# Moving one of the shifted copies of VectorE's softmax tiles to GpSimd in a planned attention + MLP kernel

## The chip, the cores and the metric

The kernel runs on one core of a Trainium2 chip. The metric is the device time of one execution in microseconds (us). The profiles show single executions; engines are called PE (TensorE matmul), PEld (TensorE weight load), DVE (VectorE), ACT (ScalarE), POOL (GpSimd) and SP (SyncE, which issues DMAs).

## What is computed

A transformer block with adaptive layer norm: 2048 rows, width 512, 32 heads of 16, an MLP of width 1376. Cut to what matters:

```
mod = silu(c) @ w_mod                        # sa, ca, ga, sb, cb, gb: six rows of 512
h = layernorm(x) * (1 + ca) + sa
q, k, v = split_heads(h @ wqkv)              # 32 heads of 16
p = softmax(q @ k.T * 16 ** -0.5)            # per head, 2048 x 2048
x = x + ga * (merge_heads(p @ v) @ wo)
h = layernorm(x) * (1 + cb) + sb
x = x + gb * (gelu(h @ w1 + b1) @ w2 + b2)   # the result
```

All inputs and the output are bf16.

## The kernel before, in words

**Runs, tiles, blocks.** The attention is cut into 32 runs, each with 512 queries x 4 heads (the last eight: 256 queries x 8 heads). A run walks over 16 key tiles of 128 keys; a key tile is four score blocks of 128 keys x 512 columns, one for each group of 32 rows of PE. Scores stand in PSUM with keys on the partitions, and after the exponential they are the moving operand of the value matmuls (`pv_op`, line 975), which add into one PSUM bank for the run (`od`). A column of ones beside V gives the softmax denominators.

**Two ways to the exponential.** ScalarE takes score blocks in groups of three and two (`qk_a`, line 837, then the Exp at line 886). VectorE takes whole key tiles (`qk_d`). For each of a tile's four blocks it makes one first pass (`ph`, line 927): it reads PSUM and writes int16 numbers whose bits, read as bf16, are a straight-line stand-in for the exponential. When the tile is whole, `shifts` (line 937 on) adds four shifted copies of it (`sh`, line 942), each one instruction over 2048 int16 columns, and the five versions go through the value matmuls with five scalings of V (the `VX` tiles, made on GpSimd at line 771), so that the errors of the five average out. A VectorE tile thus has five groups of value matmuls where a ScalarE tile has one.

**Who takes which tile.** `DKS = (2, 6, 10, 14)` are the tiles of a run that VectorE may take. ScalarE takes the twelve others and, when these are done, those of the four that VectorE has not reached (`next_tile`).

**What sets the order.** The kernel is emitted by a list scheduler that runs when the kernel is built (`Plan`). Each step is an `Op` with an engine, an assumed duration, dependencies, a priority and buffers (`Res`) to take and give back; the scheduler keeps one model clock per engine, picks at each step the op that can start first (among near ones by `dyn` and a pseudo-random term from `SEEDS`, one seed for each 25 us), and emits it. The order on each engine is fixed by that; at run time the engines wait for each other by semaphores. Where PE has nothing to do in the model, `heat` emits matmuls on zeros (lines 445, 461 and 966).

**GpSimd beside VectorE.** GpSimd work that is cut into pieces (the normalising at line 1027, the scaling of weights by their gates at line 1050) is of kind "beside": the scheduler starts a piece only when VectorE is at an op that is not marked `port` (the copies `sh` are marked, the first passes not) and that has at least 0.5 us left (`Plan.beside`). `after_dve` makes the piece wait for the VectorE instruction before the last one emitted.

**The other parts.** Layer norm, projections and MLP of the four row blocks are spread among the runs; `block_tail` does output projection, second layer norm and MLP of a row block, and `last_half` the last 256 rows after the last run. The gelu works in place on `g`; the last chunk of `g` (96 of 128 partitions are used) gets ones in its spare partitions (`ones`, line 1148), so that the last W2 matmul adds b2. `late_loads` fetches weights in the first run, among them `WoP`, two regroupings of the last rows of Wo that only `last_half` uses (line 1281).

Of the kernel before, what the change touches and what calls it, by code (L numbers as in the profile page):

```python
# [25 lines left out]
NPH = 5  # L26
# [34 lines left out]
AL = 0.055  # L61
FILL = 2.1
SPREAD = 0.15
SEEDS = (189, 218, 297, 155, 171, 163, 261, 540, 974, 172, 672, 279, 663, 728, 301, 465, 719, 329, 508, 485, 116, 24, 319, 395, 351, 431, 815, 192, 264, 111, 379, 921)
HEAT = 1.7


# [8 lines left out]
class Op:  # L76
    count = 0

    def __init__(self, eng, fn, us, deps=(), lat=0.14, prio=5.0, mode=None, kind="", acq=None,
                 rel=(), gate=None, port=False):  # L80
        self.port = port
        self.eng, self.fn, self.us, self.lat, self.prio = eng, fn, us, lat, prio
        self.mode, self.kind, self.acq, self.rel, self.gate = mode, kind, acq, rel, gate
        self.end = None
        self.ready = 0.0
        self.tile = None
        self.slot = None
        self.kb, self.due, self.extra = 0, 1e9, False
        self.uses, self.use = 0, 1.0
        self.rows, self.cont, self.run = None, False, None  # L90
        self.waiters = []
        self.todo = 0
        self.seq = Op.count
        Op.count += 1
        for d in deps:
            if d is None:
                continue
            if d.end is None:
                d.waiters.append(self)
                self.todo += 1  # L100
            else:
                self.ready = max(self.ready, d.end)
        for owner in rel:
            owner.uses += 1
# [165 lines left out]
def kernel(  # L270
# [28 lines left out]
    EPS = 1e-5  # L299
    QSC = 0.25 * 128.0 / math.log(2.0)  # L300
    ESC = math.log(2.0) / 128.0
    DKS = (2, 6, 10, 14)
    NPT = 4
    FEW = 1
    MM = 0.2155
    SPAN = (3, 2)
    POOL_US, POOL_MIN = 0.68, 0.5
    A_US = {1: 0.49, 2: 0.9165, 3: 1.3435}
    AHEAD = 3
    PSUM_F = 11  # L310
    FIRST_DKS, D_TIME = (14,), 8.0

    psum = bass.MemoryType.PSUM
# [8 lines left out]
    def res(name, n, shape, dt, pool=work):  # L322
        return Res(name, n, lambda i: pool.tile(shape, dt, name=f"{name}{i}"))
# [5 lines left out]
    r_ax = res("ax", 2, [P, QB], FP32, pp)  # L329
    r_pt = [res(f"pt{n}_", NPT, [P, n * QB], BF16) for n in SPAN]  # L330
    r_ph = res("ph", 4, [P, 4 * QB], I16)
    r_sh = res("sh", 4, [P, 4 * QB], I16)
    r_xb = res("xb", 2, [P, TPB, D], BF16)
    r_blk = res("blk", NQ, [P, NC, D], BF16)
    r_w = res("w", 3, [P, NC, D], BF16)
# [22 lines left out]
    urgent = set()  # L358
    aux_at = [0.0]

    def dyn(plan, o):
        if o.eng == "DVE" and o.run is not None and (
                o.run < a_run[0] or o.run == a_run[0] and not own[o.run]):
            return 0.05
        if o.eng != "PE":
            return o.prio
        same = (-0.5 if o.mode[0] == plan.mode else 0.0) - 0.2 * o.cont
        if o.kind == "qkA":
            back = n_a[0] - n_a[1]
# [106 lines left out]
    sc = const.tile([P, NC], BF16, name="sc")  # L476
    modA = const.tile([P, 2 * NC], FP32, name="modA")
    modB = const.tile([P, 2 * NC], FP32, name="modB")
    ga_bc = const.tile([P, D], FP32, name="ga_bc")
    gb_bc = const.tile([P, D], FP32, name="gb_bc")  # L480
    qmask = const.tile([P, 2], FP32, name="qmask")
    Wo = keep.tile([P, NC, D], BF16, name="Wo")
    WoP = keep.tile([P, 2, D], BF16, name="WoP")
# [415 lines left out]
    def qk_d():  # L899
# [24 lines left out]
        def ex(e):  # L924
            n_d[1] += 1
            units[0] += 1
            nc.vector.tensor_scalar(out=ph.tile[:, o.row * QB:(o.row + 1) * QB], in0=o.tile, scalar1=PH_B,  # L927
                                    scalar2=0.0, op0=ALU.add, op1=ALU.max)
        d_e.append(op("DVE", ex, 0.6, (o,), lat=DL, prio=0.5, rel=(o,)))
        d_e[-1].run = r  # L930
        if last:
            shifts(r, kt, ph, list(d_e))

# [3 lines left out]
    def shifts(r, kt, first, es):  # L937
        def parts(o):
            return lambda: [o.tile[:, h * QB:(h + 1) * QB].bitcast(BF16) for h in range(4)]
        pv_op(r, kt, 0, es, parts(first), (first,))  # L940
        for j in range(1, NPH):
            sh = op("DVE", lambda o, j=j: nc.vector.tensor_scalar(  # L942
                out=o.tile, in0=first.tile, scalar1=PH_SH[j], scalar2=None, op0=ALU.add),
                0.6, es, lat=DL, prio=2.0, acq=r_sh, rel=(first,), port=True)
            sh.run = r
            pv_op(r, kt, j, (sh,), parts(sh), (sh,))

    def pv_op(r, kt, ph, deps, srcs, owners):
        cc, par, hb = run_heads(r)
# [127 lines left out]
    def late_loads(after):  # L1077
# [10 lines left out]

        def wo(o):
            nc.sync.dma_start(out=Wo, in_=A_wo.rearrange("(c p) f -> p c f", p=P))  # L1090
            wo_src = A_wo[(NC - 1) * P:NC * P, :].rearrange("(r p d) f -> r p d f", r=4, p=2)
            for r in range(4):
                for p in range(2):
                    nc.sync.dma_start(out=WoP[32 * r:32 * r + 16, p, :], in_=wo_src[r, p])
        z1 = op("POOL", lambda o: nc.gpsimd.memset(WoP, 0.0), 0.9, d, prio=8.0)
        o_late["wo"] = dma(wo, (z1,), kb=640, n=9)
        z2 = op("POOL", lambda o: (nc.gpsimd.memset(W1[:, :, F:NF * P], 0.0),
                                   nc.gpsimd.memset(b1_bf, 0.0),
                                   nc.gpsimd.memset(W2c[:, 2, :], 0.0)), 1.5, d, prio=8.0)
# [14 lines left out]
                          (o_late["small"],), prio=3.0)  # L1114

    W2 = {}

    def gate_bc(dst, w, kind):
        def bc(o):
# [51 lines left out]
    def block_tail(b, nt=TPB):  # L1171
# [19 lines left out]
        if part:  # L1191
            g.uses += 1
            x2.uses += 1
            held["x"] = x2
            o_late["part"] = g
            one = ones(g, (g,))
        ev = []
        if part:
            open_banks()
# [11 lines left out]
        if part:  # L1211
            ge = [op("ACT", lambda o, lo=lo, hi=hi: nc.scalar.activation(  # L1212
                out=g.tile[:, lo:hi, 0:N], in_=g.tile[:, lo:hi, 0:N], func=ACT.Gelu_apprx_tanh),
                0.2 * (hi - lo) * nt / 2 + 0.1 + 1.3 * (lo == 0), ev[lo:hi], lat=0.15, prio=0.5,
                gate=finished) for lo, hi in ((0, 2), (2, PSUM_F))]
# [5 lines left out]
        if part:  # L1221
            due(1e9)
        prev = None
        for t in range(nt):
            mm = chain([(lambda ps, t=t, f=f: w2_mm(ps, g.tile, t * P, f, f + 1), MM)
                        for f in range(NF)], (prev, one, o_late["w2"]), "part" if part else kind, r_ax, (g,), 3,
                       lambda f: ge[0] if not part else ge[f >= 2] if f < PSUM_F else ev[f])
# [14 lines left out]
    def last_half():  # L1242
# [15 lines left out]
        for n, t in enumerate(tiles):  # L1258
# [19 lines left out]
            def wo2(o, t=t):  # L1278
                for p in range(2):
                    at = p * HB + (t % 2) * P  # L1280
                    nc.tensor.matmul(out=acc[t].tile, lhsT=OT.tile[:, at:at + P], rhs=WoP[:, p, :], start=False,
                                     stop=(p == 1))
            w = op("PE", wo2, 2 * MM, (ml, early[t]), lat=PEL, mode=full, kind="last", prio=0.2)
# [25 lines left out]
            for f in range(NF):  # L1309
                def w1(o, f=f, at=at):  # L1310
# [3 lines left out]
                mm = op("PE", w1, 4 * 0.064, hd, lat=PEL, mode=full, kind="last", acq=r_t, prio=0.3)  # L1314
                gd.append(op("ACT", lambda o, f=f, mm=mm, gs=gs: nc.scalar.activation(
                    out=g.tile[0:rows(f), f, gs], in_=mm.tile[0:rows(f), 0:P], func=ACT.Gelu_apprx_tanh,
                    bias=b1c[0:rows(f), f:f + 1], scale=1.0), 0.265, (mm,), prio=0.3, rel=(mm,)))
            first = prev = None
            for f in range(NF):
                def w2(o, f=f, gs=gs):  # L1320
                    w2_mm((first_of[id(o)] or o).tile, g.tile, gs.start, f, f + 1)
                o = op("PE", w2, MM, (gd[f], prev), lat=PEL if f == NF - 1 else 0.0, mode=full,
                       kind="last", acq=r_ax if f == 0 else None, prio=0.4)
                first_of[id(o)] = first
                first = first or o
# [40 lines left out]
    def want_q(g):  # L1366
        while q_made[0] < g and q_made[0] + 1 < NQ * NC:
# [4 lines left out]
            due(1e9)  # L1372
            if cc == NC - 1:
                o_h[b].uses -= 1

    state = {"late": 0}
    qk_a()
    want_q(1)
    while True:
# [7 lines left out]
        while ended:  # L1387
# [13 lines left out]
            if r == 0:  # L1401
                late_loads(o_last[0])
                o_late["ga"] = gate_bc(ga_bc, o_late[2], "gate")
                o_late["wo"] = scaled([lambda u=u: Wo[:, u, :] for u in range(NC)] +
                                      [lambda p=p: WoP[:, p, :] for p in range(2)], ga_bc,
                                      (o_late["wo"], o_late["ga"]))
                lt = {3: o_late[3], 4: o_late[4]}
                gt = o_late["g"]
# [15 lines left out]
            if r == 6:  # L1424
# [43 lines left out]
```

## Time and profile before

| | us |
|---|---|
| median of three runs | 783.03 (781.84 to 783.94) |
| the profiled execution | 783.1 |
| its span, first to last instruction | 781.3 |
| busy in it: PE, DVE, ACT, POOL | 746.6, 737.4, 755.3, 124.5 |
| key tiles done by VectorE | 476 first passes / 4 = 119 of 512 |

A row of the costliest groups has the line, engine, operation, tiles (out<-in), their shapes and the count, then busy us and the mean ns of one, then the engine's idle time ahead of them and what ended it. Busy time merges what overlaps, so it can be less than count times mean. In the timeline a row is a start, a length, an engine, and a count of merged neighbours. In the table by stage, each engine has its busy us in the stretch.

### The profile page before, as it was taken

Reading aid. Unit: us, or ns where it says so; the run is one execution under the profiler, and the core shown is the slowest. Engines: PE = TensorE matmul, PEld = TensorE weight load, DVE = VectorE, ACT = ScalarE, POOL = GpSimd, SP = SyncE. Lnnn points to the kernel's source line nnn. Section 1 sums busy time; section 2 is a strip of 40 time slices with the busy share of each in tenths; the row PEclk is TensorE's granted clock in tenths of the full one; section 3 lists DMA queues with packets and bytes.
Section 4 is the critical chain, followed back from the end, with each engine's and each line's share of the span. In section 5 each row is a group of like instructions: output and inputs, shape, how many; then the busy total and the mean of one; then the engine's idle time right before and its main releaser. Section 6 shows DMA issues by size and latency. Waiting matters only on the chain.

```text
span 781.3 us, 21165 instructions
## 1 busy us (share of the span) xinstructions
PE 746.6 (96%) x8617; PEld 273.2 (35%) x8617; DVE 737.4 (94%) x1288; ACT 755.3 (97%) x680; POOL 124.5 (16%) x279
## 2 busy tenths in 40 slices
PE   8999999999999999999999999999999999999997
PEld 3433333333333222223322233222233444434455
DVE  6889987999999999999999999999999999999994
ACT  4899999999999999999999999999999999999994
POOL 6611124021224300010000200000000100010100
PEclk9999999999999999999999999999999999999999
DMA  7143001100020101010100010000111101010100
GB/s 215 36 117 106 19 23 47 24 22 9 13 74 23 25 22 46 17 23 6 44 19 22 25 26 20 20 22 24 31 46 31 26 18 46 18 24 18 26 18 28
DMA packets 38547, 27.73 MB, mean 35 GB/s; under 512 B 17941, under 2 KB 33846, under 8 KB 38450
## 3 DMA queue, kind: packets, MB, share of 16 engines
q1 hardware_dynamic: 38442, 26.39, 12.5%
q8 instruction: 67, 1.10, 0.6%
q14 instruction: 30, 0.25, 0.1%
q10 hardware_dynamic: 8, 0.00, 0.0%
HBM read 20.77 MB, written 2.61 MB: 30 GB/s over the span
## 4 chain that ended last, share of the span: by engine, by line
PE 34%; DVE 28%; ACT 26%; issue 8%; DMA 2%; SPq 1%; POOL 1%; DVEq 0%; ACTq 0%
ACT pt L886 24%; DVE sh L942 11%; DVE ph L927 11%; PE od L975 11%; PE st L837 10%; PE ax L1141 3%; PE ax L837 3%; PE ax L716 2%; PE ax L1202 2%; PE od L461 1%; DVE OD L1000 1%; DVE ln_s L621 1%; PE ax L1135 1%; DMA xb<-in_A_x_dram 1%; PE ax L755 1%
## 5 line engine op out<-in xcount | busy, mean ns | idle before, releaser
L886 ACT ACTIVATE pt<-st 128x1536 bf16<-128x1536 f32 x629 | 714.2, 1308 | 2.2 <-PE st L837 1.0
L927 DVE TENSOR_SCALAR ph<-ax 128x512 int16<-128x512 f32 x476 | 310.4, 682 | 8.0 <-PE ax L837 6.8
L942 DVE TENSOR_SCALAR sh<-ph 128x2048 int16<-128x2048 int16 x476 | 312.6, 694 | 2.1 <-PE od L975 0.9
L837 PE MATMUL st<-qm,kT 32*128 32x512 bf16 x1572 | 246.4, 383 | 16.0 <-ACT pt L886 12.4
L975 PE MATMUL od<-sh,VX 128*32 128x512 bf16 (+1 forms) x2400 | 167.4, 340 | 3.6 <-DVE sh L942 2.8
L837 PE MATMUL ax<-qm,kT 32*128 32x512 bf16 x476 | 158.9, 379 | 3.3 <-DVE ph L927 1.6
L837 PEld LDWEIGHTS <-kT 32*128 32x128 bf16 x2048 | 77.2, 91 | 233.6 <-issue 224.3
L975 PE MATMUL od<-pt,VEB 128*32 128x512 bf16 (+1 forms) x1960 | 141.8, 340 | 0.1
L975 PEld LDWEIGHTS <-VX 128*32 128x32 bf16 x2400 | 60.0, 95 | 84.6 <-issue 72.9
L975 PEld LDWEIGHTS <-VEB 128*32 128x32 bf16 x2560 | 62.9, 96 | 75.5 <-issue 59.4
L1027 POOL TENSOR_TENSOR OT<-OD,RB 128x256 bf16<-128x256 f32 x38 | 27.4, 732 | 320.4 <-DVE sh L942 207.3
L975 PE MATMUL od<-ph,VEB 128*32 128x512 bf16 (+1 forms) x600 | 46.9, 338 | 1.0 <-DVE OD L1000 0.7
L1202 PE MATMUL ax<-blk,W 128*128 128x512 bf16 (+1 forms) x176 | 44.1, 355 | 0.7 <-DVE ph L927 0.4
L461 PE MATMUL od<-warm 128*32 128x512 bf16 x440 | 41.7, 381 | 0.0
L716 PE MATMUL ax<-blk,w 128*128 128x512 bf16 x124 | 36.7, 382 | 1.3 <-DVE blk L640 0.6
L771 POOL TENSOR_SCALAR VX<-VEB 128x128 bf16<-128x128 bf16 x64 | 23.6, 369 | 89.2 <-DVE VEB L647 85.5
L1027 POOL TENSOR_TENSOR OS<-OD,RB 128x256 bf16<-128x256 f32 x24 | 17.2, 729 | 127.0 <-DVE sh L942 111.7
L1141 PE MATMUL ax<-w,g 128*128 128x512 bf16 x128 | 34.6, 381 | 1.8 <-ACT g L1212 1.0
L1207 DVE TENSOR_SCALAR g<-ax,b1c 128x512 bf16<-128x512 f32 (+1 forms) x44 | 29.2, 675 | 0.3 <-PE ax L1202 0.2
L621 DVE BATCH_NORM_STATS2 ln_s<-xb 128x6 f32<-128x512 bf16 x32 | 21.7, 678 | 2.8 <-DMA xb<-in_A_x_dram 2.7
L1141 PEld LDWEIGHTS <-g 128*128 128x128 bf16 x176 | 13.9, 97 | 24.1 <-issue 12.2
L1000 DVE COPY OD<-od 128x512 f32<-128x512 f32 x31 | 21.1, 681 | 0.2 <-PE od L975 0.2
(106 smaller groups left out, 375.8 us busy)
## 6 DMA issues: line engine op xcount, KB each, us to landing
RB<-rn SPq DMA_DIRECT2D x124, 64.0 KB
xb<-in_A_x_dram SPq DMA_DIRECT2D x7, 512.0 KB
out_dram<-o SPq DMA_DIRECT2D x16, 128.0 KB
qm<-qs SPq DMA_DIRECT2D x120, 16.0 KB
W<-in_B_w_dram SPq DMA_DIRECT2D x1, 1376.0 KB
w<-in_A_wqkv_dram SPq DMA_DIRECT2D x3, 384.0 KB
blk<-in_w_mod_dram SPq DMA_DIRECT2D x2, 512.0 KB
g<-in_w_mod_dram SPq DMA_DIRECT2D x2, 512.0 KB
```

The source lines that it names most:

```text
L461: nc.tensor.matmul(out=o_od[r].tile[32 * i:32 * i + 32, :], lhsT=warm[:, 0:32], rhs=warm[:, 0:1].to_broadcast([P, QB]), start=False, stop= ...
L621: nc.vector.bn_stats(out=st6, in_=src)
L716: return chain([(lambda ps, j=j: nc.tensor.matmul(out=ps[:, 0:QB], lhsT=w.tile[:, j, cc * P:(cc + 1) * P], rhs=o_h[b].tile[:, j, :], start ...
L837: nc.tensor.matmul(out=o.tile[:, k * QB:(k + 1) * QB], lhsT=kT[cc][kb][rows, ko * P:(ko + 1) * P], rhs=qm.tile[rows, par, :] if hb is None ...
L886: nc.scalar.activation(out=e.tile[:, 0:len(got) * QB], in_=o.tile[:, 0:len(got) * QB], func=ACT.Exp, scale=ESC)
L927: nc.vector.tensor_scalar(out=ph.tile[:, o.row * QB:(o.row + 1) * QB], in0=o.tile, scalar1=PH_B, scalar2=0.0, op0=ALU.add, op1=ALU.max)
L942: sh = op("DVE", lambda o, j=j: nc.vector.tensor_scalar(out=o.tile, in0=first.tile, scalar1=PH_SH[j], scalar2=None, op0=ALU.add), 0.6, es, ...
L975: nc.tensor.matmul(out=o_od[r].tile[32 * i:32 * i + 32, n * HB:n * HB + w], lhsT=v_tile(kt, ph)[:, c0:c0 + 32], rhs=got[i][:, at:at + w], ...
L1027: two = beside(lambda c: nc.gpsimd.tensor_tensor(out=OT.tile[:, c], in0=OD.tile[:, c], in1=o5.tile[:, c], op=ALU.mult), (OT,), (OD, o5), f ...
L1141: nc.tensor.matmul(out=ps, lhsT=g[:, f, col:col + P], rhs=rhs, start=(f == 0), stop=(f == NF - 1))
L1202: mm = chain([(lambda ps, f=f, j=j, f0=f0: nc.tensor.matmul(out=ps[:, (f - f0) * N:(f - f0 + 1) * N], lhsT=W1[:, j, f * P:(f + 1) * P], rh ...
L1207: ev.append(op("DVE", lambda o, f=f, f0=f0, mm=mm: nc.vector.tensor_scalar(out=g.tile[:, f, 0:N], in0=mm.tile[:, (f - f0) * N:(f - f0 + 1) ...
```

## The change

- For a VectorE tile, the last of the four shifted copies is now made on GpSimd (`by_pool`): four pieces of 512 int16 columns, each after the first pass that it reads, of kind "beside", with 0.65 us in the model, into one buffer `sg`. This is done after 60 us of the model's clock, when at most four such pieces are pending, and, for the run that ScalarE is at, when at least six tiles of it are left. Otherwise VectorE makes the copy as before.
- VectorE alternates: after a first pass, a ready copy comes before the next first pass (`d_last`, `ALT`).
- `DKS` has five tiles (2, 5, 8, 11, 14), so there are 20 VX tiles for 16; three `sh` buffers for four; the gates `ga_bc` and `gb_bc` in bf16.
- `WoP` has no tile of its own any more: its memset, eight loads and four scalings come at run 24 into a buffer of `r_w` (`split_wo`).
- The row of ones is written behind the gelu for all row blocks, and the last W2 matmul waits for it.
- `SEEDS` is another list.

The diff, cut to its core:

```
-SEEDS = (189, 218, 297, 155, ...
+SEEDS = (925, 529, 257, 846, ...
...
-    DKS = (2, 6, 10, 14)
+    DKS = (2, 5, 8, 11, 14)
...
+    G_US, G_MIN, G_PRIO, G_MAX, G_FROM, G_TILES = 0.65, 0.5, 1.0, 4, 60.0, 6
...
-    r_sh = res("sh", 4, [P, 4 * QB], I16)
+    NSG = 1
+    r_sh = res("sh", 3, [P, 4 * QB], I16)
...
+    d_last = [False]
+    ALT = 0.4
+
     def dyn(plan, o):
...
+        if o.eng == "DVE" and o.alt and d_last[0]:
+            return ALT
...
-    ga_bc = const.tile([P, D], FP32, name="ga_bc")
-    gb_bc = const.tile([P, D], FP32, name="gb_bc")
+    ga_bc = const.tile([P, D], BF16, name="ga_bc")
+    gb_bc = const.tile([P, D], BF16, name="gb_bc")
...
         for j in range(1, NPH):
-            sh = op("DVE", lambda o, j=j: nc.vector.tensor_scalar(
-                out=o.tile, in0=first.tile, scalar1=PH_SH[j], scalar2=None, op0=ALU.add),
-                0.6, es, lat=DL, prio=2.0, acq=r_sh, rel=(first,), port=True)
-            sh.run = r
+            if j == NPH - 1 and g_left[0] <= G_MAX and plan.now > G_FROM and (
+                    r > a_run[0] or len(own[r]) + len(shared[r]) >= G_TILES):
+                by_pool(r, kt, j, first, es, parts)
+                continue
+            def shift(o, j=j):
+                d_last[0] = False
+                nc.vector.tensor_scalar(out=o.tile, in0=first.tile, scalar1=PH_SH[j], scalar2=None, op0=ALU.add)
+            sh = op("DVE", shift, 0.6, es, lat=DL, prio=2.0, acq=r_sh, rel=(first,), port=True)
+            sh.run, sh.alt = r, True
             pv_op(r, kt, j, (sh,), parts(sh), (sh,))
+
+    g_left = [0]
+    r_sg = res("sg", NSG, [P, 4 * QB], I16)
+
+    def by_pool(r, kt, j, first, es, parts):
+        sh = op("NIL", None, 0.0, es[:1], lat=0.0, prio=0.0, acq=r_sg)
+        got = []
+        for h in range(4):
+            def go(o, e=es[h]):
+                g_left[0] -= 1
+                c = slice(e.qk.row * QB, (e.qk.row + 1) * QB)
+                after_dve(nc.gpsimd.tensor_scalar(
+                    out=sh.tile[:, c], in0=first.tile[:, c], scalar1=1.0, scalar2=float(PH_SH[j]),
+                    op0=ALU.mult, op1=ALU.add))
+            g_left[0] += 1
+            got.append(op("POOL", go, G_US, (sh, es[h]), lat=0.1, prio=G_PRIO, kind="beside", rel=(first,), port=True,
+                          gate=lambda: plan.beside(G_MIN)))
+        pv_op(r, kt, j, got, parts(sh), (sh,))
...
-        z1 = op("POOL", lambda o: nc.gpsimd.memset(WoP, 0.0), 0.9, d, prio=8.0)
-        o_late["wo"] = dma(wo, (z1,), kb=640, n=9)
+        o_late["wo"] = dma(wo, d, kb=512)
...
+    def split_wo():
+        held["wop"] = wop = op("NIL", None, 0.0, (), lat=0.0, prio=0.0, acq=r_w)
...
+        z1 = op("POOL", lambda o: nc.gpsimd.memset(wop.tile[:, 0:2, :], 0.0), 0.9, (wop,), prio=1.0)
+        ld = dma(load, (z1,), kb=128, n=8, prio=3.0)
+        o_late["wop"] = scaled([lambda p=p: wop.tile[:, p, :] for p in range(2)], ga_bc, (ld,))
...
-            one = ones(g, (g,))
...
-            one = ones(g, ge)
+        one = ones(g, ge)
...
+            if r == LAST * 8:
+                split_wo()
```

More of the change, by code (lines that the diff above doesn't have):

```diff
@@ L63 @@
 SPREAD = 0.15
-SEEDS = (189, 218, 297, 155, 171, 163, 261, 540, 974, 172, 672, 279, 663, 728, 301, 465, 719, 329, 508, 485, 116, 24, 319, 395, 351, 431, 815, 192, 264, 111, 379, 921)
+SEEDS = (925, 529, 257, 846, 939, 899, 560, 662, 544, 155, 536, 522, 19, 893, 450, 795, 742, 2, 4, 794, 818, 153, 176, 144, 484, 633, 742, 123, 569, 63, 333, 698)
 HEAT = 1.7
@@ L88, in __init__ @@
         self.kb, self.due, self.extra = 0, 1e9, False
-        self.uses, self.use = 0, 1.0
+        self.uses, self.use, self.alt = 0, 1.0, False
         self.rows, self.cont, self.run = None, False, None
@@ L307 @@
     POOL_US, POOL_MIN = 0.68, 0.5
+    G_US, G_MIN, G_PRIO, G_MAX, G_FROM, G_TILES = 0.65, 0.5, 1.0, 4, 60.0, 6
     A_US = {1: 0.49, 2: 0.9165, 3: 1.3435}
     AHEAD = 3
-    PSUM_F = 11
     FIRST_DKS, D_TIME = (14,), 8.0
@@ L478 @@
     modB = const.tile([P, 2 * NC], FP32, name="modB")
-    ga_bc = const.tile([P, D], FP32, name="ga_bc")
-    gb_bc = const.tile([P, D], FP32, name="gb_bc")
+    ga_bc = const.tile([P, D], BF16, name="ga_bc")
+    gb_bc = const.tile([P, D], BF16, name="gb_bc")
     qmask = const.tile([P, 2], FP32, name="qmask")
     Wo = keep.tile([P, NC, D], BF16, name="Wo")
-    WoP = keep.tile([P, 2, D], BF16, name="WoP")
     W1 = keep.tile([P, NC, NF * P], BF16, name="W1")
@@ L926, in ex @@
             units[0] += 1
+            d_last[0] = True
             nc.vector.tensor_scalar(out=ph.tile[:, o.row * QB:(o.row + 1) * QB], in0=o.tile, scalar1=PH_B,
@@ L929, in qk_d @@
         d_e.append(op("DVE", ex, 0.6, (o,), lat=DL, prio=0.5, rel=(o,)))
-        d_e[-1].run = r
+        d_e[-1].run, d_e[-1].qk = r, o
         if last:
@@ L1090, in wo @@
             nc.sync.dma_start(out=Wo, in_=A_wo.rearrange("(c p) f -> p c f", p=P))
[L1091 to L1094, printed above, removed]
-        z1 = op("POOL", lambda o: nc.gpsimd.memset(WoP, 0.0), 0.9, d, prio=8.0)
-        o_late["wo"] = dma(wo, (z1,), kb=640, n=9)
+        o_late["wo"] = dma(wo, d, kb=512)
         z2 = op("POOL", lambda o: (nc.gpsimd.memset(W1[:, :, F:NF * P], 0.0),
@@ L1116, with load @@
     W2 = {}
+    def split_wo():
+        held["wop"] = wop = op("NIL", None, 0.0, (), lat=0.0, prio=0.0, acq=r_w)
+        def load(o):
+            wo_src = A_wo[(NC - 1) * P:NC * P, :].rearrange("(r p d) f -> r p d f", r=4, p=2)
+            for r in range(4):
+                for p in range(2):
+                    nc.sync.dma_start(out=wop.tile[32 * r:32 * r + 16, p, :], in_=wo_src[r, p])
+        z1 = op("POOL", lambda o: nc.gpsimd.memset(wop.tile[:, 0:2, :], 0.0), 0.9, (wop,), prio=1.0)
+        ld = dma(load, (z1,), kb=128, n=8, prio=3.0)
+        o_late["wop"] = scaled([lambda p=p: wop.tile[:, p, :] for p in range(2)], ga_bc, (ld,))
     def gate_bc(dst, w, kind):
@@ L1214, in block_tail @@
                 0.2 * (hi - lo) * nt / 2 + 0.1 + 1.3 * (lo == 0), ev[lo:hi], lat=0.15, prio=0.5,
-                gate=finished) for lo, hi in ((0, 2), (2, PSUM_F))]
+                gate=finished) for lo, hi in ((0, 2), (2, NF))]
         else:
@@ L1219, in block_tail @@
                 0.1 + 1.2 * nt + 2.6, ev, lat=-1.2, prio=0.5)]
-            one = ones(g, ge)
+        one = ones(g, ge)
         if part:
+            o_late["one"] = one
             due(1e9)
@@ L1225, in block_tail @@
             mm = chain([(lambda ps, t=t, f=f: w2_mm(ps, g.tile, t * P, f, f + 1), MM)
-                        for f in range(NF)], (prev, one, o_late["w2"]), "part" if part else kind, r_ax, (g,), 3,
-                       lambda f: ge[0] if not part else ge[f >= 2] if f < PSUM_F else ev[f])
+                        for f in range(NF)], (prev, o_late["w2"]) + (() if part else (one,)), "part" if part else kind, r_ax, (g,), 3,
+                       lambda f: ge[0] if not part else one if f == NF - 1 else ge[f >= 2])
             prev = mm
@@ L1280, in wo2 @@
                     at = p * HB + (t % 2) * P
-                    nc.tensor.matmul(out=acc[t].tile, lhsT=OT.tile[:, at:at + P], rhs=WoP[:, p, :], start=False,
+                    nc.tensor.matmul(out=acc[t].tile, lhsT=OT.tile[:, at:at + P], rhs=held["wop"].tile[:, p, :], start=False,
                                      stop=(p == 1))
-            w = op("PE", wo2, 2 * MM, (ml, early[t]), lat=PEL, mode=full, kind="last", prio=0.2)
+            w = op("PE", wo2, 2 * MM, (ml, early[t], o_late["wop"]), lat=PEL, mode=full, kind="last", prio=0.2)
             a = op("DVE", lambda o, t=t: nc.vector.tensor_tensor(
@@ L1316, in last_half @@
                     out=g.tile[0:rows(f), f, gs], in_=mm.tile[0:rows(f), 0:P], func=ACT.Gelu_apprx_tanh,
-                    bias=b1c[0:rows(f), f:f + 1], scale=1.0), 0.265, (mm,), prio=0.3, rel=(mm,)))
+                    bias=b1c[0:rows(f), f:f + 1], scale=1.0), 0.265, (mm, g), prio=0.3, rel=(mm,)))
             first = prev = None
@@ L1321, in w2 @@
                     w2_mm((first_of[id(o)] or o).tile, g.tile, gs.start, f, f + 1)
-                o = op("PE", w2, MM, (gd[f], prev), lat=PEL if f == NF - 1 else 0.0, mode=full,
+                o = op("PE", w2, MM, (gd[f], prev) + ((o_late["one"],) if f == NF - 1 else ()), lat=PEL if f == NF - 1 else 0.0, mode=full,
                        kind="last", acq=r_ax if f == 0 else None, prio=0.4)
@@ L1374, in want_q @@
                 o_h[b].uses -= 1
+            if q_made[0] + 1 == NQ * NC:
+                o_w[0].uses -= 1
     state = {"late": 0}
@@ L1403 @@
                 o_late["ga"] = gate_bc(ga_bc, o_late[2], "gate")
-                o_late["wo"] = scaled([lambda u=u: Wo[:, u, :] for u in range(NC)] +
-                                      [lambda p=p: WoP[:, p, :] for p in range(2)], ga_bc,
+                o_late["wo"] = scaled([lambda u=u: Wo[:, u, :] for u in range(NC)], ga_bc,
                                       (o_late["wo"], o_late["ga"]))
```

## The prediction

> **What bounds the kernel now.** I read the page's busy shares first, then busy time by stage, then the costliest groups, then the timeline around single GpSimd pieces, because the change puts work on GpSimd beside VectorE.
>
> ```profile
> 0.00:60.00 60.00, 54.24 (x497) 23.08 (x498) 46.16 (x99) 47.14 (x48) 27.32 (x113) 1.00 0.43 125
> 60.00:200.00 140.00, 134.53 (x1478) 46.98 (x1481) 131.05 (x228) 139.98 (x125) 30.61 (x60) 1.00 0.13 34
> 200.00:400.00 200.00, 190.36 (x2059) 61.82 (x2051) 198.61 (x338) 199.20 (x176) 35.27 (x58) 1.00 0.11 29
> 400.00:600.00 200.00, 194.42 (x2009) 61.73 (x2005) 196.19 (x331) 199.57 (x170) 15.22 (x22) 1.00 0.09 26
> 600.00:740.00 140.00, 136.64 (x2102) 58.38 (x2103) 137.12 (x239) 139.89 (x120) 13.01 (x20) 1.00 0.10 25
> 740.00:781.30 41.30, 36.46 (x490) 21.23 (x482) 28.22 (x58) 29.55 (x46) 3.07 (x6) 1.00 0.08 22
> ```
>
> The columns are stretch, length, then busy us of PE, weight loads, VectorE (DVE), ScalarE (ACT) and GpSimd (POOL), the granted clock, DMA. From 60 to 740 us ACT is busy 678.6 of 680 us and DVE 663.0: both are full, and a key tile can be computed by either. PE is busy 656.0, but 38.8 us of that is line 461, matmuls on zeros that the planner throws in where PE has nothing better; they can give way. GpSimd is busy 94.1 us of 680. The clock is 1.00 in every stage. So the middle is a division of key tiles between two full engines; what counts is the VectorE time of a tile.
>
> ```profile
> L886 ACT ACTIVATE pt<-st 128x1536 bf16<-128x1536 f32 x629 | 714.2, 1308 | 2.2 <-PE st L837 1.0
> L927 DVE TENSOR_SCALAR ph<-ax 128x512 int16<-128x512 f32 x476 | 310.4, 682 | 8.0 <-PE ax L837 6.8
> L942 DVE TENSOR_SCALAR sh<-ph 128x2048 int16<-128x2048 int16 x476 | 312.6, 694 | 2.1 <-PE od L975 0.9
> L771 POOL TENSOR_SCALAR VX<-VEB 128x128 bf16<-128x128 bf16 x64 | 23.6, 369 | 89.2 <-DVE VEB L647 85.5
> ```
>
> An ACT tile is four score blocks: 714.2 us for 1572 blocks is 0.454 each, 1.815 us a tile. A VectorE tile is four first passes (L927) and four shifted copies (L942), so 476 of each are 119 tiles, 113 of them between 60 and 740 us (453 and 454 instructions). Neighbours overlap a little: three first passes in a row take 1.89 us in the timeline, so each after the first adds 0.60 us, and in the timeline every plain step between two of these instructions is 0.602. A tile costs VectorE 8 x 0.602 = 4.82 us.
>
> **What a GpSimd piece does to VectorE.** Pieces of the normalising step (L1027) already run beside first passes:
>
> ```profile
> 492.51 0.68 DVE L942 TENSOR_SCALAR sh<-ph 128x2048 int16<-128x2048 int16 x1
> 493.11 0.68 DVE L927 TENSOR_SCALAR ph<-ax 128x512 int16<-128x512 f32 x1
> 493.27 0.73 POOL L1027 TENSOR_TENSOR OS<-OD,RB 128x256 bf16<-128x256 f32 x1 [20.29 <-DVE sh L942]
> 493.71 0.84 DVE L942 TENSOR_SCALAR sh<-ph 128x2048 int16<-128x2048 int16 x1
> 494.47 0.74 DVE L1207 TENSOR_SCALAR g<-ax,b1c 128x512 bf16<-128x512 f32 x1
> ```
>
> The piece waits for the copy before the first pass and starts 0.16 us after that pass does. It ends at 494.00, and the copy that follows takes 0.84 instead of 0.68: the next instruction starts 0.76 after it instead of 0.60. Where a first pass follows, nothing is lost: two pieces from 288.36 on lie beside three first passes that take the plain 1.89. Over all copies that follow such pieces one line fits: the copy is lengthened by (piece's end minus copy's start) minus 0.133. With the start at 0.16 and the copy at 0.60 the stall is D - 0.573, D being the piece's duration: 0.155 at 0.73, and 0.10 for the 0.676 us pieces of L1050, whose copies take 0.786. **D decides this change.**
>
> **Part 1, the copy on GpSimd.** For most tiles after 60 us the last of four copies becomes four GpSimd tensor_scalar pieces, 128x512 int16. VectorE loses 0.602 us a tile, and gains the stalls. No row shows this piece. From below: a memset of 512 columns (L1099) takes 525 ns, so D is 0.525 and there is no stall. From above: line 771, the same operation on 128 columns, 369 ns; with 0.22 for two columns (L626) that is 1.15 ns a column, and 0.22 + 510 x 1.15 = 0.81. That row walks runs of 16 columns, whereas the new pieces are contiguous like the memsets, whose slope is (525 - 207)/384 = 0.83 ns (L439, L1099): 0.22 + 510 x 0.83 = 0.64. I take 0.65, nearer the contiguous rows. The planner enters 0.65 for it as well; its entries that the trace can check are near (0.6 for VectorE against 0.602, 0.68 for the old pieces against 0.676 to 0.73).
>
> By alternation each first pass is followed by a copy as long as there are copies: three copies on four first passes, so three of the four pieces stall one. Stall 0.65 - 0.573 = 0.077; saved per tile 0.602 - 3 x 0.077 = 0.371.
>
> [...]
>
> How many tiles: one sg buffer. Four first passes with a copy and a stall between take 4 x 1.28 = 5.1 us, with the last piece and the matmuls that read the buffer about 6.0. A VectorE tile comes each 680/113 = 6.0 us now, and about 5.6 after. So the buffer allows some 93%; G_MAX (over four pieces pending: VectorE copies as before) and the guard for the end of a run take a little more. I take 100 of 113: 100 x 0.371 = 37 us of VectorE time.
>
> **Part 2, what 37 us are worth.** DKS offers five tiles a run instead of four, and ScalarE takes what VectorE does not reach, so tiles move until both end together. One tile moved costs VectorE 4.82 less 0.88 x 0.371, 4.49 us, and frees 1.815 on ACT. 37 / (4.49 + 1.815) = 5.9 tiles; ACT and the span lose 5.9 x 1.815 = 10.7 us. That rate, 0.29 us of span for 1 us of VectorE, prices every VectorE term below.
>
> **Part 3, PE.** A moved tile adds four value groups (eight matmuls in two groups last 0.62, four 0.40: 0.22 a group), and four single score blocks of 0.22 in place of 1.6 groups: 0.88 + 0.53 = 1.41, for 5.9 tiles 8.3 us. The cover is 24 us of PE idle time and 38.8 of zeros between 60 and 740. Cost nothing; without that cover up to 8 us.
>
> **Part 4, the rest.** The fifth tile of DKS brings 16 scalings (0.369) and 12 memsets to GpSimd, some 9 us on an engine that is 86% idle in the middle; copies beside the present ones last 0.68 to 0.83, so four groups cost VectorE under 0.6 us, 0.2 of span. Gates in bf16, three sh buffers for four (with three copies a tile for four): nothing, with a wait for a buffer as the risk. WoP's memset, eight loads and four scalings move from the first run to run 24; the first run's SP queue gets shorter, and at run 24 eight issues of about 0.5 us stand before the RB loads of one run, which the pieces of L1027 wait for, and those have a run's time. The row of ones is set behind the gelu: 0.5 us (L1148) hidden by the eight W2 matmuls of 0.22 that do not need it; without them 0.6 us once. Seeds and alternation reorder a middle in which ACT is idle 1.4 us: little to win. ACT's mean step is 1.345 and 0.924 against medians of 1.331 and 0.904, some 10 us in 620; I take 0, bounds -3 to +3.
>
> Sum: 783.1 (the profiled execution: span 781.3 and 1.8 around it; the median of three runs is 783.03, the same) - 10.7 = **772.4 us**.
>
> **Rivals.**
> *The piece is long (slower).* If D is the 0.81 of the strided row, the stall is 0.238, three are 0.71, more than the 0.602 saved: each tile loses 0.11, 100 lose 11 us, tiles go back to ACT and the time is 783.1 + 3.0 = 786.1. The turn is at D = 0.573 + 0.602/3 = 0.774. For it: line 771 is the same operation. Against: the contiguous memsets. Chance 0.16.
> *No stall.* D at or under 0.573, near the memset's 0.525: 0.602 a tile, 60 us, 60/(4.29 + 1.815) x 1.815 = 17.9, 765. Chance 0.14.
> *PE waits for the late piece.* The plan has a piece end 0.65 + 0.1 after the first pass starts; by the rows it is 0.16 + 0.65. PE runs in order, and where the fourth copy's matmuls come at once, 0.06 us a tile, 6 us in all, delays the scores behind them for ACT, which has no slack: 778. Chance 0.13. Against: PE has several value groups to choose from.
> *It does less than it says.* Buffer, gate and G_MAX let a third through: 34 x 0.371 = 12.6, 3.5 us of span, 779.6. Chance 0.09.
> The forecast itself, 767 to 778: 0.48.
>
> **Numbers.** 0.3% of 783 is 2.35 us, about what a measurement of this kernel can tell from no change. Faster: 0.48 + 0.14 + 0.09 (PE) + 0.05 (a third) = 0.76; within: 0.04 + 0.04 + 0.03 of the long piece = 0.11; slower: the other 0.13 of it. Range 764 to 786, which cuts the ends of the short and the long piece.
>
> **What would show it.** The GpSimd row of the new line: about 400 pieces, mean near 0.65 (0.77 or more: the slower rival). Copies after a piece near 0.76 us. About 500 first passes and 400 copies on VectorE; ACT's group near 620 instructions; line 461 shrunk; DVE and ACT still full from 60 to 730 us. Idle time of PE put down to the GpSimd pieces would speak for the third rival. Wrong altogether if ACT shows idle time in the middle, or VectorE does.

## The result and the profile after

The changed kernel takes 785.17 us (median of six runs, 784.81 to 785.81) against 782.6 us of the kernel before: a ratio of 1.0034, 95% interval 1.0021 to 1.0046. It is slower by 0.3%, where 1.4% faster was forecast; the time lies inside the stated range, at its upper end. The profiled execution took 785.1 us, its span is 783.2.

These are the stages of the kernel after, with the columns of the same table before (stretch, length, then busy us of PE, weight loads, DVE, ACT and POOL, the granted clock, DMA):

```profile
60.00:200.00 140.00, 135.15 (x1473) 47.79 (x1466) 121.12 (x208) 139.52 (x125) 66.39 (x123) 1.00 0.11 27
200.00:400.00 200.00, 190.08 (x2014) 59.37 (x2015) 195.33 (x326) 198.49 (x175) 94.91 (x156) 1.00 0.12 30
400.00:600.00 200.00, 193.16 (x2044) 62.01 (x2036) 191.02 (x317) 197.09 (x167) 77.64 (x122) 0.99 0.09 26
600.00:740.00 140.00, 134.01 (x2040) 57.28 (x2032) 132.06 (x224) 137.80 (x118) 59.60 (x92) 1.00 0.10 26
```

From 60 to 740 us VectorE is now busy 639.5 us, where it was 663.0: it is idle 40.5 us instead of 17. ACT is busy 672.9 instead of 678.6. Neither is full any more, and the clock is no longer 1.00 in every stage. The costliest groups of the kernel after (line, engine, operation, tiles, shapes, count, then busy us and mean ns, then idle time before and its releaser):

```profile
L891 ACT ACTIVATE pt<-st 128x1536 bf16<-128x1536 f32 x624 | 710.8, 1302 | 8.3 <-PE st L842 5.7
L933 DVE TENSOR_SCALAR ph<-ax 128x512 int16<-128x512 f32 x488 | 321.9, 679 | 25.0 <-PE ax L842 22.0
L969 POOL TENSOR_SCALAR sg<-ph 128x512 int16<-128x512 int16 x332 | 205.3, 627 | 306.1 <-DVE sh L954 201.1
L954 DVE TENSOR_SCALAR sh<-ph 128x2048 int16<-128x2048 int16 x405 | 284.4, 723 | 4.1 <-PE od L1004 2.9
L1004 PE MATMUL od<-sg,VX 128*32 128x512 bf16 (+1 forms) x424 | 34.4, 338 | 0.4 <-POOL sg L969 0.3
```

Read from the top: ACT has 624 groups for 629, that is 1560 score blocks for 1572, three key tiles less. VectorE has 488 / 4 = 122 tiles for 119, the same three. GpSimd makes 332 / 4 = 83 fourth copies, each piece 0.627 us. The copies left on VectorE last 723 ns on average, 29 more than before. ACT waits 8.3 us ahead of its exponentials (2.2 before), VectorE 25.0 us ahead of its first passes (8.0 before), 22.0 of it for scores from PE. PE itself waits only 0.3 us for the GpSimd pieces.

### The profile page after: what moved, and what is told of

The parts are those of the page before. It is cut to its first block, busy times and chain, and to the rows that moved or that the text cites. A ratio compares the mean times of both kernels' runs of the same rounds, so it can differ in the third digit from the quotient of the medians.

```text
span 783.2 us, 21425 instructions
## 1 busy us (share of the span) xinstructions
PE 746.6 (95%) x8547; PEld 270.9 (35%) x8547; DVE 715.4 (91%) x1229; ACT 752.0 (96%) x675; POOL 337.3 (43%) x639
## 5 line engine op out<-in xcount | busy, mean ns | idle before, releaser
L933 DVE TENSOR_SCALAR ph<-ax 128x512 int16<-128x512 f32 x488 | 321.9, 679 | 25.0 <-PE ax L842 22.0
L969 POOL TENSOR_SCALAR sg<-ph 128x512 int16<-128x512 int16 x332 | 205.3, 627 | 306.1 <-DVE sh L954 201.1
L954 DVE TENSOR_SCALAR sh<-ph 128x2048 int16<-128x2048 int16 x405 | 284.4, 723 | 4.1 <-PE od L1004 2.9
L842 PE MATMUL ax<-qm,kT 32*128 32x512 bf16 x488 | 170.2, 379 | 3.9 <-DVE ph L933 2.5
L1004 PE MATMUL od<-sh,VX 128*32 128x512 bf16 (+1 forms) x2024 | 145.3, 342 | 5.9 <-DVE sh L954 5.2
L1004 PE MATMUL od<-ph,VEB 128*32 128x512 bf16 (+1 forms) x612 | 48.6, 340 | 1.2 <-DVE OD L1029 1.1
L776 POOL TENSOR_SCALAR VX<-VEB 128x128 bf16<-128x128 bf16 x80 | 27.6, 346 | 39.6 <-DVE VEB L652 35.0
L1004 PE MATMUL od<-sg,VX 128*32 128x512 bf16 (+1 forms) x424 | 34.4, 338 | 0.4 <-POOL sg L969 0.3
L467 PE MATMUL od<-warm 128*32 128x512 bf16 x320 | 31.5, 388 | 0.0
```

The costliest lines, as they stand in the source:

```text
L467: nc.tensor.matmul(out=o_od[r].tile[32 * i:32 * i + 32, :], lhsT=warm[:, 0:32], rhs=warm[:, 0:1].to_broadcast([P, QB]), start=False, stop= ...
L842: nc.tensor.matmul(out=o.tile[:, k * QB:(k + 1) * QB], lhsT=kT[cc][kb][rows, ko * P:(ko + 1) * P], rhs=qm.tile[rows, par, :] if hb is None ...
L954: nc.vector.tensor_scalar(out=o.tile, in0=first.tile, scalar1=PH_SH[j], scalar2=None, op0=ALU.add)
L969: after_dve(nc.gpsimd.tensor_scalar(out=sh.tile[:, c], in0=first.tile[:, c], scalar1=1.0, scalar2=float(PH_SH[j]), op0=ALU.mult, op1=ALU.add))
L1004: nc.tensor.matmul(out=o_od[r].tile[32 * i:32 * i + 32, n * HB:n * HB + w], lhsT=v_tile(kt, ph)[:, c0:c0 + 32], rhs=got[i][:, at:at + w], ...
```

## The experiments

Theory A is contention: the order is good, and GpSimd's pieces hold up VectorE's copies, which PE and ACT then feel. Theory B is the order: VectorE's freed time cannot be used, because scores do not come any earlier. Theory C is the draw: the time of any one list of seeds scatters by several us. Theory D, which one of the runs tests, is that the alternation starves VectorE. "The port" is named after the planner's mark `port`: in the planner's model a copy on VectorE and a piece on GpSimd do not run at the same time. In the expectations "the scheduler's own model" is the clock on which the kernel's planner lays out its order when it is built; it ends at 775.6 us for the kernel before and at 770.6 for the changed one.

**The same order with short pieces.**

```
-                    out=sh.tile[:, c], in0=first.tile[:, c], scalar1=1.0, ...
+                    out=sh.tile[:, c][:, 0:32], in0=first.tile[:, c][:, 0:32], scalar1=1.0, ...
...
```

The lines left out fill the buffer once with zeros, by a GpSimd memset ahead of the first piece.

> The changed kernel with the same order on every engine, but each GpSimd piece of the fourth copy writes 32 of its 512 columns (the other columns of the copy stay as one memset left them, so 15/16 of that copy is left out). Theory A, contention: the order is good and what ate the gain is GpSimd holding the shared access: stalled copies on VectorE (13.5 us in all, copies 723 ns on average) and late small GpSimd steps, which PE and ACT then wait for. Copies fall back to about 0.69 us, ACT's idle time between its exponentials falls from 8.3 us toward 2, and the time falls by 5 us or more, to 776 to 780. Theory B, order: VectorE waits for scores because PE gives them at a fixed order that has no more to offer; copies fall to 0.69 us as well, but VectorE's idle time ahead of its first passes grows by the same 13 us and the time stays within 1.5 us of 785.2.

Measured 776.95 us, ratio 0.9929 (0.9914 to 0.9944). The exponentials, the first passes, the copies and the pieces of this kernel:

```profile
L891 ACT ACTIVATE pt<-st 128x1536 bf16<-128x1536 f32 x624 | 708.1, 1322 | 2.5 <-PE st L842 1.6 <-PE ax L842 0.5
L933 DVE TENSOR_SCALAR ph<-ax 128x512 int16<-128x512 f32 x488 | 324.0, 683 | 27.5 <-PE ax L842 24.8 <-PE st L842 0.9
L954 DVE TENSOR_SCALAR sh<-ph 128x2048 int16<-128x2048 int16 x405 | 272.8, 695 | 4.4 <-PE od L1004 3.4
L969 POOL TENSOR_SCALAR sg<-ph 128x32 int16<-128x32 int16 x332 | 73.3, 222 | 404.8 <-DVE sh L954 235.2 <-DVE ph L933 41.0 <-PE ax L842 29.2
```

The copies are back at 695 ns, and with the same order and the same 122 tiles the time falls by 8.2 us. ACT waits 2.5 us ahead of its exponentials instead of 8.3. Theory A holds for most of it: this order is worth 5.5 us against the kernel before (782.45 in these runs), and what the long pieces do took 8.2. VectorE still waits for scores (24.8 us, and 27.5 in all ahead of first passes), so part of theory B holds too: the freed time is not used.

**Pieces of 448 and of 256 columns**, the same edit with other sizes.

> The changed kernel with the same order, each GpSimd piece cut from 512 to 448 columns (an eighth of the fourth copy is left out; the other columns stay as one memset left them). A piece then lasts about 0.57 us, just the length at which the line from before says a copy behind it is not stalled. If the stall of the next copy decides: copies fall to about 0.69 us and the time to 777 to 779, though GpSimd is nearly as busy as before. If it is GpSimd being occupied (its layer-norm steps coming late): little is won, 782 to 785.

> As e5_448 with 256 of 512 columns (half of the fourth copy is left out), about 0.42 us a piece. If the stall decides: the same as with 448 and with 32 columns, 776.5 to 778.5. If occupation of GpSimd decides: half way between 785 and 777, 780 to 782.

Measured 783.01 (ratio 1.0005, 0.9996 to 1.0015; ten runs from 781.9 to 784.8) and 779.0 (0.9955, 0.9940 to 0.9970). First the copies and the pieces with 448 columns, then the copies with 256:

```profile
L954 DVE TENSOR_SCALAR sh<-ph 128x2048 int16<-128x2048 int16 x405 | 280.4, 714 | 4.2 <-PE od L1004 3.1
L969 POOL TENSOR_SCALAR sg<-ph 128x448 int16<-128x448 int16 x332 | 188.7, 573 | 315.6 <-DVE sh L954 190.2 <-PE od L1004 23.2 <-PE st L842 21.7
```

```profile
L954 DVE TENSOR_SCALAR sh<-ph 128x2048 int16<-128x2048 int16 x405 | 273.2, 696 | 4.5 <-PE od L1004 3.4
```

Neither time lies where the expectation for stalls alone had it. With 448 columns a piece lasts 0.573 us and the copies 714 ns, not the 690 that I expected: I had every piece start 0.16 us after its first pass, and here half of them start 0.23 or later. The line itself holds to the end. Summed over the copies that follow a piece, (piece's end minus copy's start) minus 0.133 gives 11.3 us in the changed kernel and 8.3 with 448 columns; measured are 11.6 and 8.2, against 0.683 us for a copy that nothing lengthens. So with 448 columns most of the stall was still there. With 256 columns the copies are at 696, as with 32, but 2 us of time stay: part of the loss is not in the copies. One part that the traces show is VectorE's wait for the small layer-norm steps on GpSimd (line 637 for line 633): 4.0 us in the changed kernel and with 448 columns, 3.1 with 256, 1.9 with 32.

**Letting the port hold the piece.** Five pieces of the changed kernel had begun while a copy still ran; each lasts over 1 us and ends 0.47 to 0.48 us after the copy, where the others typically end 0.70 after it (the median). One of them:

```profile
468.23 0.66 DVE L954 TENSOR_SCALAR sh<-ph 128x2048 int16<-128x2048 int16 x1
468.25 1.11 POOL L969 TENSOR_SCALAR sg<-ph 128x512 int16<-128x512 int16 x1 [1.24 <-DVE ln_s L626]
468.81 0.68 DVE L933 TENSOR_SCALAR ph<-ax 128x512 int16<-128x512 f32 x1
```

So here a piece that is already waiting when the copy ends is done some 0.2 us sooner. The edit makes it wait for the VectorE instruction one place earlier in the order; nothing is left out:

```
-    def after_dve(pool):
+    def after_dve(pool, n=1):
...
-        if len(own) > 1:
-            tc.add_manual_dep(pool.ins, own[1].name, ...
+        if len(own) > n:
+            tc.add_manual_dep(pool.ins, own[n].name, ...
...
-                    op0=ALU.mult, op1=ALU.add))
+                    op0=ALU.mult, op1=ALU.add), 2)
```

> The changed kernel, same order, whole work; the new GpSimd pieces wait for the VectorE instruction one place earlier (the third last emitted in place of the second last), so that a piece is issued while the copy ahead of the first pass still runs and lets the port itself hold it. The five pieces of the changed kernel that were held so ended 0.477 us after the copy, against some 0.70 for the others. Theory A: pieces show over 1 us, copies fall to about 0.69 us, and the time falls to 777 to 780. Rival: a piece that comes early gets the port ahead of a copy and holds VectorE for most of its length; copies over 1 us in the tens, and 786 or more.

> As e7_early, with the earlier wait for all pieces beside VectorE, those of the normalising and of the weight scaling too (some 100 more). Theory A: another 0.5 to 1.5 us below e7_early. Rival: more pieces get the port first, above e7_early.

Measured 777.36 (ratio 0.9933, 0.9919 to 0.9948) and 777.17 (0.9932, 0.9915 to 0.9948): both faster than the kernel before, with the whole work; between the two there is no difference that these runs can tell, so the second expectation is not borne out. The copies fall to 698 and 691 ns, and VectorE's wait for the layer-norm steps to 1.9 us in both. First the timeline of VectorE and GpSimd in the changed kernel, then the same instructions in e7_early:

```profile
300.33 0.68 DVE L933 TENSOR_SCALAR ph<-ax 128x512 int16<-128x512 f32 x1
300.60 0.62 POOL L969 TENSOR_SCALAR sg<-ph 128x512 int16<-128x512 int16 x1 [1.08 <-PE ax L842]
300.93 0.83 DVE L954 TENSOR_SCALAR sh<-ph 128x2048 int16<-128x2048 int16 x1
```

```profile
298.67 0.68 DVE L954 TENSOR_SCALAR sh<-ph 128x2048 int16<-128x2048 int16 x1
298.91 0.92 POOL L969 TENSOR_SCALAR sg<-ph 128x512 int16<-128x512 int16 x1 [0.50 <-DVE ph L933]
299.27 0.68 DVE L933 TENSOR_SCALAR ph<-ax 128x512 int16<-128x512 f32 x1
299.87 0.68 DVE L954 TENSOR_SCALAR sh<-ph 128x2048 int16<-128x2048 int16 x1
```

The piece looks longer (0.92 us, part of it waiting behind the copy of 298.67) but ends at 299.83, before the next copy begins, and that copy takes 0.68 instead of 0.83. The rival, pieces that get the port first, hardly shows: seven copies over 1 us, against nine in the changed kernel.

**The draw of the order.** The lists of seeds are exchanged between the two kernels, then the alternation is taken out (`ALT = 2.0`).

> The changed kernel with the seeds of the kernel before. Theory A (contention eats the gain whatever the order): 785 give or take 2. Theory C, the draw of the order: each list of seeds is one draw whose time scatters by several us, so that part of any result is the draw; the scheduler's own model ends 8 us later with these seeds, so 790 to 795.

> The kernel before with the seeds of the changed one. Theory C: a draw like any other, the scheduler's model ends 5 us later with them, so 786 to 790, which says how much of the time of before is its own draw. If seeds do not matter (against theory C): 782 to 784.

> The changed kernel with the alternation off (a copy has its old priority 2.0 after a first pass too). Theory D, alternation starves VectorE: more first passes come in a row, VectorE's idle time ahead of them falls below the 25 us of the changed kernel, and the time is under 783. Theory C: only another draw; the scheduler's model ends 9 us later than with alternation, so 790 to 795, and the idle time does not fall.

Measured 791.44 (ratio 1.0111, 1.0094 to 1.0128), 788.02 (1.0074, 1.0059 to 1.0089) and 795.0 (1.0163, 1.0148 to 1.0178). A list alone moves the time by 5 to 6 us, so each kernel owes that much to its own list, and the one before too. It also sets how many tiles VectorE gets: with the old list 119 in the kernel before and 120 in the changed one, with the new list 118 and 122. Theory D falls: without alternation the wait ahead of first passes rises to 33.1 us. What alternation itself is worth is not settled by that run: in its trace the clock is at half for 10.2 us in one place, and ACT falls about 8 us further behind the scheduler's model there.

**The earlier wait in another order.**

> e2_old_seeds (791.4) with the earlier wait of e7_early, so the same test of contention in another order. Theory A: it falls by 6 to 9 us here too, to 782 to 786. If the 8 us were a property of one order: 788 to 791.

Measured 789.15 (ratio 1.0078, 1.0060 to 1.0095): 2.3 us less than e2_old_seeds, not the 6 to 9 expected. The copies went from 722 to 703 ns, 7.6 us over 400 of them. So what a us of longer copies goes with depends on the order: 0.3 us here, 7.8 / 10.1 = 0.8 from the changed kernel to e7_early (405 copies, 723 to 698 ns), where the 7.8 us also hold the later layer-norm steps and a drop of the clock (below). The sign is the same in both. With the earlier wait in place, one list for both kernels gives 788.02 to 777.36 us with the new list and 782.99 to 789.15 with the old one. That the first pair differs by just the 10.7 us of the forecast is chance: four tiles moved in it, not 5.9, and the second pair goes the other way. So the 5.3 us by which e7_early beats the kernel before, each with its own list, are partly a draw, and what the change is worth in any order is not settled.

**What else VectorE waits for.** e7_early without nearly all value matmuls of the fourth copy (408 of 424; `out` marks that copy, and the last group of a run keeps its matmuls):

```
...
-                for i in range(4):
+                for i in range(0 if out and not first and left[r] else 4):
...
```

> e7_early with the same order, less the value matmuls of the copy that GpSimd makes (one fifth of the work of 83 tiles is left out, some 18 us of PE). VectorE is idle 42 us of the middle in e7_early, 24 of them waiting for scores from PE. If PE's load is what keeps VectorE from its scores: that wait falls from 24 us to under 14. If the waits come from the order and the two score banks, not from load: it stays over 20. ACT is full in e7_early, so the time can fall little either way: 775 to 777.5.

Measured 776.72 (ratio 0.9917, 0.9902 to 0.9932). PE's busy time from 60 to 740 us falls from 654.7 to 638.5, and VectorE's waits stay. Waits of e7_early, then of this kernel (engine and line, who is waited for, us, times, longest):

```profile
DVE ph L933 <- PE ax L842: 24.0, 41, 2.4
```

```profile
DVE ph L933 <- PE ax L842: 24.3, 42, 2.4
```

It is not the load of these matmuls. What PE saves it waits for ACT instead: its waits ahead of ACT's scores go from 11.4 to 20.8 us. The waits of VectorE are part of the order in which the scores are issued: in e7_early PE is idle for 0.6 us of them only, and otherwise busy with matmuls that stand ahead. Which rule of the scheduler puts them there was not found.

**Without the copy on GpSimd** (`G_FROM = 1e9`), all other edits kept:

> The changed kernel without the copy on GpSimd (VectorE makes all four), with alternation, five tiles on offer, three buffers and the other edits kept, and the seeds of before (with its own list the scheduler finds no order). The theory that the gain of the order comes from the copy on GpSimd alone: the other edits are no help without it, 795 to 806, since three buffers hold fewer copies than a tile has. If they matter little: 783 to 792, as another draw of the kernel before.

Measured 813.1 (ratio 1.0392, 1.0356 to 1.0428): far slower, beyond what I expected. ACT waits 27.4 us, 18.4 of it for value matmuls, and the clock is at half for 23.9 us in three places. Three copy buffers with four copies a tile could explain it, but that is not shown: this is one order, and the clock's part was not separated.

**A searched list.** Four seeds of e8_early_all changed.

> e8_early_all with four of its 32 seeds changed, found by trying lists against the scheduler's own model, which ends 1.5 us earlier. If the model is followed as in e8_early_all: 775 to 776.5. If the draw on the chip is as large as the gain: 776 to 779.

Measured 777.42 (ratio 0.9926, 0.9912 to 0.9941): no better than 777.17. 1.5 us in the model are less than it can be trusted for.

## Why the prediction was wrong

**The piece: right.** D was taken as 0.65 us; it is 0.627, with 0.573 for 448 columns, 0.412 for 256 and 0.222 for 32: 0.84 ns a column and 0.195 us fixed. The slower rival's 0.81 is refuted. It also rested on a misreading: the 369 ns of line 771 is a mean, in which eleven instructions count that lie beside a copy of VectorE and last 0.62 to 0.75 us; 52 of the 64 take 0.303, which is what the line of 0.84 ns a column gives for 128 columns.

**The stall: the line right, the size near by luck, and less often.** 0.077 us was taken per piece for three pieces in four. 138 of 332 pieces are followed by a copy, and those copies are 0.084 us longer on average, 11.6 us in all. The line holds; it was read off several pieces of the kernel before. That 0.084 is so near 0.077 is partly luck: 92 of the 138 pieces start about 0.16 us after the first pass, as assumed, and lengthen the copy by 0.058, while the other 46 start 0.2 us after it or later and lengthen it by 0.136. The hold-up goes both ways in the trace of the changed kernel: the copy of 300.93 lasts 0.83 us behind a piece, where a copy with no GpSimd instruction beside it takes 0.68 (the median of 210), and the piece of 468.25 lasts 1.11 us behind a copy, where the median piece takes 0.62. By what the two engines hold each other up no trace shows.

**The number of tiles: 83 for 100.** Together with the smaller stall it gives 83 x 0.602 - 11.6 = 38 us of VectorE time, where the prediction had 37.

**What 37 us are worth: this step failed, twice.** First, "tiles move until both end together" did not happen. The prediction had named the sign of this itself, idle time of VectorE in the middle. Three tiles moved, not 5.9, and 23.5 us of the freed time became idle time. ACT lost 3 x 1.815 = 5.4 us of work, and that is what this order brings: e7_early, nearly free of stalls, is 5.3 us faster than the kernel before, and the scheduler's own model gains 5.0 (775.6 to 770.6). With the same list in both kernels one tile or four move, never the 5.9. The rate assumed two engines with tiles always at hand; here VectorE's first passes wait for scores that come in the order of the list, and e9_no_fourth_pv shows that taking the fourth copy's matmuls off PE does not bring them sooner.

Second, the same rate, 0.29 us of span per us of VectorE, was put on the stalls. It holds where tiles can be divided anew; but the division is fixed when the kernel is built, and a stall at run time is lateness, which passes to PE, whose order is fixed, and so to ACT, which has little slack (672.9 of 680 us busy). By that rate the 10.1 us of longer copies between the changed kernel and e7_early would cost 2.9 us; the time differs by 7.8. Against the scheduler's model the kernel before ends 7.0 us later and e7_early 6.8, the changed kernel 14.6. Together, 5.3 us won by the order and 7.8 lost make the changed kernel 2.5 us slower, and 2.6 is measured. One can follow it in two traces with one order, by how much later the same exponential begins in the changed kernel: 0.2 us near 49, 0.6 near 247, 2.4 near 360 and near 453, 4.9 near 481, 6.2 near 658 and 7.6 at the last.

**The jump near 473 us**, 2.5 of the 7.6, is a chain that the prediction had not seen. The waits in the changed kernel's timeline:

```profile
469.41 0.68 DVE L954 TENSOR_SCALAR sh<-ph 128x2048 int16<-128x2048 int16 x1
469.45 0.72 POOL L631 TENSOR_SCALAR rs<-mv 128x2 f32<-128x2 f32 x1
470.25 0.71 POOL L633 TENSOR_TENSOR rs<-rs,mhalf 128x2 f32<-128x2 f32 x1
470.99 0.73 DVE L637 TENSOR_SCALAR z<-xb,mv,rs 128x512 bf16<-128x512 bf16 x2 [0.90 <-POOL rs L633]
472.38 0.38 PE L699 MATMUL ax<-ident,z 128*128 128x128 bf16 x4 [1.51 <-DVE ph L933]
473.30 1.45 ACT L891 ACTIVATE pt<-st 128x1536 bf16<-128x1536 f32 x1 [0.81 <-PE st L842]
```

and the stages of that moment (PE's busy us is the first figure after the length, the clock the figure after the POOL column):

```profile
470.90:472.40 1.50, 0.02 (x1) 0.02 (x1) 1.41 (x4) 1.50 (x2) 0.64 (x2) 1.00 0.00 0
472.90:476.30 3.40, 3.40 (x28) 1.18 (x26) 2.87 (x6) 1.54 (x2) 0.00 (x0) 0.50 0.00 0
```

The held piece of 468.25 makes the small layer-norm steps on GpSimd late, and the first of them then lies behind the copy of 469.41 as well (0.72 us, where the same step takes 0.22 undisturbed). VectorE waits 0.90 us for them, PE 1.51 us for VectorE, and after that gap the clock is at half for 3.4 us, so that ACT waits again. In e7_early the clock stays at 1.00. The trace of e5_448 parts the two: it has the same chain with the same gap of 1.51 us near 470 us, but the clock stays at 1.00, and the lateness against e7_early grows there by 0.9 us only. So the half clock is worth about 1.5 of the 2.5 us, and the gap alone does not bring it about. There is one profile of the changed kernel, but all six of its executions on record have a mean granted clock of 0.998, which is what one stretch of 3.4 us at half clock in 783 us comes to; at what place the five others have it is not shown.

**The rivals.** "PE waits for the late piece" is refuted as it was put (0.3 us of waits), though the way it named, PE's fixed order passing lateness on to ACT, is the one that decided, with VectorE's copies as the late party. "No stall" at 765 was wrong in its price: nearly without stalls the time is 777. "It does less than it says" is refuted in its condition, a third of the copies: GpSimd makes 83 of them. PE's added load cost little, as forecast: with 16 us less of PE's work e9_no_fourth_pv is 0.6 us faster than e7_early. The draw of the order was priced at -3 to +3 us; it is worth 5 to 6.

## What to carry to other kernels

In a kernel with a fixed order, do not price a stall by what a new division of the work would make of it: what the order did not allow for goes down the engines' fixed queues, and went here with 0.3 to 0.8 us per us of longer copies (the 0.8 with a drop of the clock in it, about 0.6 without). If a planner lays out the order, read its own forecast too: here it gained 5.0 us where the division by hand gave 10.7. Time freed on one of two full engines is worth something only so far as the order hands that engine more work, so count the work that moves, not the time that comes free. Before a difference of a few us between two such kernels is put down to a change, give both the same list, and more than one. And where instructions of two engines lengthen each other, as the copies and the pieces do here, try issuing the second one early instead of having it wait for a semaphore: in e7_early the piece of 298.91 so ends 0.48 us after its copy, where those of the changed kernel typically end 0.70 after it, and the time is 777.36 us for 785.17; with the other list it is 789.15 for 791.44.

## What was unexpected of the hardware

In the changed kernel the five GpSimd pieces held behind a VectorE copy ended 0.47 to 0.48 us after that copy, and the pieces that waited for the copy's completion typically 0.70 after it (the median), so 0.2 us is won by issuing them early. And 1.51 us of idle PE were followed by a granted clock of 0.50 for 3.4 us in the changed kernel, whose PE is 95% busy, while the same gap of 1.51 us in e5_448 was followed by a clock of 1.00; what decides between the two was not found.
